# The first four chunks of a recurrence inverted in one batch, their loads first, and eight PSUM banks for attention until the first block

## The chip, the cores and the metric

The kernel runs on one core of one Trainium2 chip. Times are device microseconds of that core; the median of three runs is what is compared (before: 1098.84 us, runs from 1097.51 to 1099.29). Five engines work on one program, each with its own list of instructions that it takes strictly in order: PE (TensorE, matrix products), DVE (VectorE), ACT (ScalarE), POOL (GpSimd) and SP (SyncE, which here only issues DMAs). They wait for one another by semaphores.

## The reference

The output is three things in a row. First a recurrence over 768 steps for 4 x 8 heads, each with a state of 40 x 40; then two feed-forward layers over 3072 tokens of 320 numbers, with 2048 hidden units each.

```python
for t in range(S):                                    # S = 768, D = 40
    y[:, :, t] = einsum('bhd,bhde->bhe', rt, state)
    Sa = einsum('bhde,bhe->bhd', state, at)
    state = state * wt[:, :, None, :] - einsum('bhd,bhe->bhde', Sa, bt) \
            + einsum('bhd,bhe->bhde', vt, kt)
x = y.transpose(0, 2, 1, 3).reshape(B * S, H * D)     # 3072 x 320
h = x @ w_in;  g = h * tanh(softplus(h));  x = g @ w_out   # first layer
h = x @ w_in;  g = h * cos(h);             out = g @ w_out # second layer
```

The weights of both layers come as 64-bit floats and are split in the kernel into a rounded part and a rest, so that each product of the layers is a sum of three matmuls: rounded input by rounded weight, rounded by rest, and rest by rounded.

## The kernel before, in words

**Recurrence.** The 768 steps are cut into 24 time chunks of 32 steps, and the heads into two halves of 16 units each. One half of one chunk is a piece g (g = 2 x chunk + half), 48 pieces in all. Inside a piece the recurrence is turned into products and the inverse of a triangular 32 x 32 matrix for each unit. A piece goes through these stages:

- `pre(g)`: the load of the inputs (IN, L564/L565), on DVE a running product of the decays (tile PE, L570), its reciprocal (D1R, L575, L576), scaled inputs (AM L584, KB L590); on PE the products of L607 and the transposes of L640; on DVE the masked results (AM, L617); a DMA stores the triangular matrix to DRAM (l_d, L630/L631).
- `inverse(bt)`: for a batch of pieces, 64 partitions for two pieces. DMA XM<-l_d (L667), then 28 dependent steps (L682 a product into XT, L680 a sum into XM; 14 of each), DMA t_d<-XM (L693), DMA TT<-t_d (L697). The steps of the first three batches are on DVE, those of later ones on POOL. All 24 batches have two pieces.
- `halves(bt)`: the two 16 x 16 blocks of each inverse are joined: TA on DVE (L724), products L719 and L721 on PE with TB (L727) between them, and a copy to TT.
- `chain(g)`: what must run from chunk to chunk, since each needs the state (SV) that the one before left: on PE the products rhs (L790), ztm (L813), zmm (L804), rvz (L862), fmm (L888) and the transposed state stm (L932); on DVE between them FR (L872), the new state SV (L899) and the output Y (L907); ACT copies RS, ZS and FL.

After two chunks, 64 steps by 4 sequences, 256 tokens are stored to DRAM (x_d, L951/L952) and make one block of the first layer.

**Layers.** Block: load XR (L1041 to L1043), rounded part XH on ACT (L1046), rest XL on DVE (L1048), hidden products h on PE (L991), activation on ACT (L1061, L1063), its rest GL on DVE (L1066), output products (L972). There are twelve such blocks, and the pieces' work runs beside them. The second layer (L1006 to L1149) comes after the last piece.

**Weights.** `prep` loads 64-bit pieces of the weights (TMP<-in_w_in, L454), ACT takes one part (L461), DVE another with two or three integer operations (L466, L471, L479), ACT or DVE writes the rounded weight (L390, L392), and POOL the rest (L508).

**Order.** A planner (`Plan`, lines 120 to 250) puts every instruction of every engine in order at build time: it simulates the engines with costs of its own, and among the work that could start it takes the lowest rank `prio`. Chains have the rank -1e4 + 10g, `pre` and `inverse` about -5e3 + 10g, the first layer 100 x block, the second layer's weights 5e3. Buffers are rings with fixed counts: PSUM's eight banks are four for attention (PA), two for h (PH) and two for outputs (PO). On the chip each engine then waits at each instruction until its inputs and its buffer are there, and all behind it in that engine's list wait too.

Of the kernel before, what the change touches and what calls it, by code (L numbers as in the profile page):

```python
# [19 lines left out]
C = 32  # L20
# [68 lines left out]
SP_SAFE = 1.0  # L89

# [8 lines left out]
class Plan:  # L99
# [23 lines left out]
    def run(self):  # L123
# [12 lines left out]
        port_free = 0.0  # L136
# [4 lines left out]
        while done < len(self.tasks):  # L141
# [88 lines left out]
            t.end = free[e] + (0.2 if t.lat is None else t.lat)  # L230
# [6 lines left out]
            for u in t.succ:  # L237
                for x in u.engs:
                    u.ready[x] = max(u.ready[x], free[e] + (HOP.get((e, x), 0.15) if t.lat is None else t.lat))
# [12 lines left out]
def body(ctx, tc, ins, out):  # L252
# [11 lines left out]
    BATCH = [(i, 2) for i in range(0, TOT, 2)]  # L264
# [141 lines left out]
    DMA_LAT = 3.0  # L406
# [6 lines left out]
    AHEAD_W = 6  # L413
# [8 lines left out]
    W1_AFTER = lambda: None  # L422
    W2_PRIO = 5e3
# [8 lines left out]
    def prep(layer, names, prio, after, stage, stage2, half):  # L432
# [7 lines left out]
        for (kind, k, cc), h, n in parts:  # L440
            late = kind == "out" and cc >= 5
            if late and t_sw is None:
# [12 lines left out]
                       preds=after + ([t_sw] if late else []) + loads[-AHEAD_W:][:1] * (len(loads) >= AHEAD_W),  # L455
                       acq=[(rring, (key, "r"))], lat=DMA_LAT + 1.5, prio=prio)
# [85 lines left out]
    Gev, KBe, scanT, ldma, ttld, tt_last, ytask = {}, {}, {}, {}, {}, {}, {}  # L542
    io, Sev, STev, chain_last = {}, {}, {}, {}
# [9 lines left out]
    def pre(g):  # L553
# [5 lines left out]
        pe, am, kb, rp = (lambda: PE_t[P.at(k("PE"))]), (lambda: AM_t[P.at(k("AM"))]), \  # L559
# [13 lines left out]
        t_sc = fifo("scan", P.add("DVE", 0.64, scan, preds=[t_ld, S_D], acq=[("PE", k("PE"))], prio=pr, port=True))  # L573
# [59 lines left out]
        ldma[g] = P.add("SP", 1.0, ldm, preds=t_gl, lat=DMA_LAT, prio=pr)  # L633
# [19 lines left out]
    def inverse(bt):  # L653
# [4 lines left out]
        rows = lambda: slice(64 * P.at(("X", bt)), 64 * P.at(("X", bt)) + 2 * n)  # L658
# [10 lines left out]
        t = P.add("SP", 1.0, ld, preds=[ldma[g0 + i] for i in range(cnt)] + [S_X], acq=[("X", ("X", bt))], lat=DMA_LAT, prio=pr)  # L669

        own = bt >= 3
        IE = G if own else V

# [17 lines left out]
        def st():  # L691
# [3 lines left out]
        t = P.add("SP", 1.0, st, preds=[t], rel=[("X", bt)], lat=DMA_LAT, prio=pr)  # L695
        t = P.add(
            "SP", 0.5, lambda: SP.dma_start(TT_t[P.at(("TT", bt))][:, 0:cnt * 4], t_d[bt].rearrange("(cg i) j t -> (i j) cg t", i=4)),  # L697
            preds=[t], acq=[("TT", ("TT", bt), cnt)], lat=DMA_LAT, prio=pr)
        t = halves(bt, t)
        for i in range(cnt):  # L700
            ttld[g0 + i] = t

    def halves(bt, t):

        g0, cnt = BATCH[bt]
# [66 lines left out]
    def chain(g):  # L772
# [142 lines left out]
        sevs, yevs = [], []  # L915
        for h, ft in ((0, f0), (1, f1)):
            s = []
            if not last:
                s = [P.add("DVE", 0.315, sev(h, p), preds=[ft, io[nx][2]], prio=pr) for p in range(2)]
            sevs += s  # L920
            rel = [k(f"F{h}")] + ([k("PE")] if h == 1 else [])
            y_acq = [("Y", ykey)] if (yc == 0 and h == 0) else []
            yevs.append(P.add("DVE", 0.26, yev(h), preds=[ft] + s + yevs, acq=y_acq, rel=rel, prio=pr + 1))
# [22 lines left out]
        if yc == 1:  # L946
# [7 lines left out]
            ytask.setdefault(yb, []).append(P.add("SP", 1.0, yst, preds=yevs, rel=[ykey], lat=DMA_LAT, prio=pr))  # L954
# [79 lines left out]
    def layer1(blk, wready):  # L1034
        pr0 = blk * 100
        xk = ("x1", blk)
        xr = lambda: XR_t[P.at((xk, "xr"))]

# [6 lines left out]
        t = P.add("SP", 1.5, ld, preds=ytask[blk] + [blk_prev[0]], acq=[("XR", (xk, "xr"))], lat=DMA_LAT, prio=pr0)  # L1045
# [297 lines left out]
```

## Time and profile before

| what | value |
|---|---|
| runs | 1097.51 to 1099.29 us, median 1098.84 us |
| the profiled execution | 1094.35 us |
| its span, first to last instruction | 1092.6 us |
| PE, DVE, ACT, POOL busy | 92%, 68%, 50%, 40% of the span |
| granted TensorE clock, mean | 0.990 of 2.4 GHz |
| first product of the first layer | 132.96 us |
| first output product of the first layer | 142.4 us |
| last product of the chain | 590.6 us |

Times inside a row are microseconds from the start of the span. The profiled execution is 1.75 us longer than its span and 4.5 us shorter than the median of the runs. Shares over the whole span mix three parts: a start in which PE is busy a third of the time, a middle with attention and the first layer together, and the second layer alone.

### The profile page before, as it was taken

The page shows a single profiled execution, that of the slowest core. Times are in us where ns is not written, and L with a number is a line of the kernel's source. Part 1 is how long each engine was busy: PE and PEld are TensorE (multiplying, and loading weights), DVE is VectorE, ACT ScalarE, POOL GpSimd, SP SyncE. Part 2 cuts the span into 40 slices and gives each one's busy share as a digit, 9 for nine tenths or more (in the row PEclk, how much of TensorE's full clock was granted, in tenths as well). Part 3 has the DMA queues.
Part 4 walks back from the last instruction along what each step waited for, and adds up shares of the span by engine and source line. Part 5 has one row for each costly group of instructions (what it writes and reads, how often), then busy time and mean ns, then how long its engine had stood idle before and what let it go on. Part 6 is the DMA issues. An engine that isn't in the chain of part 4 may idle for free.

```text
span 1092.6 us, 36346 instructions
## 1 busy us (share of the span) xinstructions
PE 1008.8 (92%) x14888; PEld 926.3 (85%) x14888; DVE 743.6 (68%) x1661; ACT 545.2 (50%) x1346; POOL 437.3 (40%) x887
## 2 busy tenths in 40 slices
PE   2266899999999999999999999999999999999996
PEld 1255798898988898889999999999999999999996
DVE  8999887778677677678643987445555555565553
ACT  3255666655565565646565444444343434343433
POOL 5215267552463754365530332103333333333332
PEclk9999799999999999999999999999999999999999
DMA  8555564646545555555443442211100202010101
GB/s 239 152 152 159 158 179 126 170 121 178 143 127 159 142 157 144 147 151 156 107 130 110 142 143 86 86 46 30 42 13 1 54 1 53 1 39 1 25 1 25
DMA packets 109367, 111.88 MB, mean 102 GB/s; under 512 B 64145, under 2 KB 88721, under 8 KB 109201
## 3 DMA queue, kind: packets, MB, share of 16 engines
q1 hardware_dynamic: 109200, 109.57, 36.9%
q8 instruction: 117, 1.92, 0.8%
q14 instruction: 50, 0.40, 0.1%
HBM read 91.43 MB, written 18.09 MB: 100 GB/s over the span
## 4 chain that ended last, share of the span: by engine, by line
PE 62%; DVE 12%; issue 11%; POOL 6%; DMA 5%; ACT 4%; SPq 1%; POOLq 0%; DVEq 0%; ACTq 0%
PE bank L991 15%; PE bank L972 15%; PE bank L1006 8%; PE bank L1022 7%; POOL GL L1149 4%; PE bank L888 4%; PE bank L862 2%; PE bank L607 1%; PE bank L932 1%; PE bank L836 1%; PE bank L640 1%; DVE SV L899 1%; PE bank L790 1%; PE bank L804 1%; PE bank L719 1%
## 5 line engine op out<-in xcount | busy, mean ns | idle before, releaser
L1149 POOL TENSOR_TENSOR GL<-H,GH 128x512 fp32r<-128x512 f32 x96 | 124.5, 1297 | 238.2 <-ACT GH L1147 228.5
L682 POOL TENSOR_TENSOR XT<-XM 64x14 f32<-64x14 f32 (+6 forms) x294 | 102.2, 348 | 176.2 <-DMA XM<-l_d 155.3
L390 ACT ACTIVATE FL<-bank 64x160 f32<-64x160 f32 (+1 forms) x376 | 101.7, 295 | 87.4 <-PE bank L932 47.1
L1140 ACT ACTIVATE T<-T,half_pi 128x512 f32<-128x512 f32 x96 | 69.5, 723 | 113.8 <-DVE T L1137 113.8
L1133 DVE TENSOR_SCALAR T<-bank 128x512 f32<-128x512 f32 x96 | 66.4, 692 | 78.5 <-PE bank L1006 65.2
L1066 DVE TENSOR_TENSOR GL<-H,GH 128x512 fp32r<-128x512 f32 x96 | 70.7, 740 | 70.8 <-ACT GH L1063 70.2
L680 POOL TENSOR_TENSOR XM<-XM,XT 64x14 f32<-64x14 f32 (+6 forms) x294 | 106.1, 361 | 22.5
L1061 ACT ACTIVATE H<-bank 128x512 f32<-128x512 f32 x96 | 57.5, 599 | 105.4 <-PE bank L991 104.7
L1142 DVE TENSOR_TENSOR H<-bank,T 128x512 f32<-128x512 f32 x96 | 66.1, 689 | 53.0 <-ACT T L1140 52.2
L1147 ACT ACTIVATE GH<-H 128x512 fp32r<-128x512 f32 x96 | 60.6, 631 | 73.1 <-DVE H L1142 71.0
L991 PE MATMUL bank<-XH,wih 128*128 128x256 f32 x448 | 94.4, 293 | 0.5 <-ACT GH L1063 0.4
L991 PE MATMUL bank<-XH,wil 128*128 128x256 f32 x448 | 89.4, 281 | 0.0
L991 PE MATMUL bank<-XL,wih 128*128 128x256 f32 x448 | 89.1, 281 | 0.0
L607 PE MATMUL bank<-AM,KB 104*64 104x64 f32 x768 | 36.9, 246 | 48.1 <-DVE KB L590 39.6
L617 DVE TENSOR_TENSOR AM<-bank,maskG 64x128 f32<-64x128 f32 x192 | 55.1, 287 | 31.4 <-PE bank L607 20.2
L607 PEld LDWEIGHTS bank<-AM,KB 104*64 104x64 f32 x768 | 30.5, 155 | 52.5 <-issue 38.6
L991 PEld LDWEIGHTS bank<-XH,wih 128*128 128x128 f32 x448 | 69.8, 191 | 2.5 <-ACT GH L1063 0.8
L991 PEld LDWEIGHTS bank<-XL,wih 128*128 128x128 f32 x448 | 69.1, 190 | 1.0 <-issue 1.0
L991 PEld LDWEIGHTS bank<-XH,wil 128*128 128x128 f32 x448 | 69.3, 191 | 0.0
L991 PE MATMUL bank<-XH,wix 128*128 128x256 f32 x224 | 67.4, 301 | 0.9 <-issue 0.9
L1137 DVE SCALAR_TENSOR_TENSOR T<-T,bank 128x512 f32<-128x512 f32 x96 | 65.7, 684 | 2.2
L888 PE MATMUL bank<-FR,FL 104*64 104x72 f32 x1536 | 63.7, 240 | 3.6 <-ACT wih L390 2.0
(171 smaller groups left out, 2929.5 us busy)
## 6 DMA issues: line engine op xcount, KB each, us to landing
VR<-in_vR_dram SPq DMA_DIRECT2D x96, 160.0 KB
IN<-in_inT_dram SPq DMA_DIRECT2D x94, 161.4 KB
FR<-in_rI_dram SPq DMA_DIRECT2D x48, 180.0 KB
FR<-in_vF_dram SPq DMA_DIRECT2D x48, 144.0 KB
TMP<-in_w_in_dram SPq DMA_DIRECT2D x12, 512.0 KB
RA<-in_w_in_dram SPq DMA_DIRECT2D x12, 512.0 KB
RA<-in_w_out_dram SPq DMA_DIRECT2D x10, 512.0 KB
SV<-in_vS_dram SPq DMA_DIRECT2D x96, 52.0 KB
```

The costliest lines, as they stand in the source:

```text
L390: A.activation(o, i, AF.Copy)
L607: PE.matmul(gp[c0:c0 + 64, q // 2], kb()[:, q].rearrange("p a t -> p (a t)"), am()[0:104, :, q], start=True, stop=True)
L680: IE.tensor_tensor(out=b[:, 0:i, i + 1:16], in0=b[:, 0:i, i + 1:16], in1=tv, op=ALU.add)
L682: IE.tensor_tensor(out=tv, in0=bc(b[:, i:i + 1, i + 1:16], (2 * n, i, w)), in1=bc(b[:, 0:i, i:i + 1], (2 * n, i, w)), op=ALU.mult)
L888: PE.matmul(fp[64 * p:64 * p + 64, qp], fl()[0:104, n * D:n * D + 64], fr()[:, n], start=True, stop=True)
L972: PE.matmul(o, l[:, f, tsl], r, start=(first and f == 0 and i == 0), stop=(last and f == 1 and i == 2))
L991: PE.matmul(hp[:, f], pss[i][0], pss[i][1], start=(i == 0), stop=(i == 7))
L1006: PE.matmul(bank[P.at((key, "h"))][:, 0:512], pss[i][0], pss[i][1], start=(i == 0), stop=(i == 7))
L1022: PE.matmul(o, l, r, start=(ft == 0 and i == 0), stop=(ft == NFF - 1 and i == 2))
L1066: gl = P.add(GLE, (dve(512),), lambda eng, Hv=Hv, key=key: EN[eng].tensor_tensor(out=GL_t[P.at((key, "gl"))], in0=Hv(), in1=GH_t[P.at((key ...
L1140: c = P.add("ACT", act(512, False, 1), lambda f=f, Tv=Tv: A.activation(Tv(f), Tv(f), AF.Sin, scale=-TWO_PI, bias=half_pi), preds=[b], aset ...
L1149: gl = P.add("POOL", pool(512), lambda f=f, Hv=Hv, key=key: G.tensor_tensor(out=GL_t[P.at((key, "gl"))], in0=Hv(f), in1=GH_t[P.at((key, "g ...
```

## The change

- **Batches.** The first inverse takes four pieces (128 partitions), the others two as before: 23 inverses in place of 24. The first two (`OWN`) are on DVE, the rest on POOL. `halves` and the tile TT still take two pieces each, so the first inverse has two TT loads. Its four `pre` come first in the program.
- **Loads.** The inputs of the first pieces stand first in SP's list. Each weight load waits in the planner for an input load (the first four) or for the third TT load (the others), and only two weight loads may be open at a time in place of six. The state, FR and VR loads of a piece wait in the planner for those of the piece before. The planner's latency of a DMA is now worked out from its size in a queue (`kb`, `RATE`, `LAND`).
- **Banks.** Attention has all eight PSUM banks until the load of the first layer's first block; four of them then go to PH and PO. The piece g = 7 keeps its tile PE in an output buffer of the first layer.
- **Ranks.** The load, XH and XL of block 0 get the rank -9.955e3, that of the chains; Y goes ahead of SV in the pieces of chunk 1.

```diff
-    BATCH = [(i, 2) for i in range(0, TOT, 2)]
+    BATCH = [(0, 4)] + [(i, 2) for i in range(4, TOT, 2)]
...
-                 ("PA", 4), ("PH", 2), ("PO", 2)):
+                 ("PA", 8), ("PH", 0), ("PO", 0)):
...
-    AHEAD_W = 6
+    OWN = 2
+    AHEAD_W = 2
+    W1_FREE = 4
...
-                       preds=after + ([t_sw] if late else []) + loads[-AHEAD_W:][:1] * (len(loads) >= AHEAD_W),
-                       acq=[(rring, (key, "r"))], lat=DMA_LAT + 1.5, prio=prio)
+                       preds=(after if layer == 2 else [tt_ld[2]] if len(loads) >= W1_FREE else [t_in[2]]) + ([t_sw] if late else []) + (loads[-AHEAD_W:][:1] * (len(loads) >= AHEAD_W) if len(loads) >= W1_FREE else loads[-1:]),
+                       acq=[(rring, (key, "r"))], kb=0.5 * n, prio=prio)
...
-        t_ld = fifo("ld", P.add("SP", 1.0, ld, preds=[S_IN[2]] if g == 1 else S_IN[0:2], acq=[] if g == 1 else [("IN", k("IN"))], lat=DMA_LAT + 1.5, prio=pr))
+        t_ld = P.add("SP", 0.8, ld, preds=[S_IN[(0, 2, 1)[g]]] if g < 3 else [t_in[g - 1]], acq=[] if g == 1 else [("IN", k("IN"))], kb=500, prio=pr if g > 3 else g - 1e6)
...
-        own = bt >= 3
+        own = bt >= OWN
...
+        prx = -9.955e3 if blk == 0 else pr0
...
-        t = P.add("SP", 1.5, ld, preds=ytask[blk] + [blk_prev[0]], acq=[("XR", (xk, "xr"))], lat=DMA_LAT, prio=pr0)
+        t = P.add("SP", 1.5, ld, preds=ytask[blk] + [blk_prev[0]], acq=[("XR", (xk, "xr"))], kb=384, prio=prx)
+        if blk == 0:
+            for i, r in enumerate(("PH", "PO", "PH", "PO")):
+                P.add("SP", 0.0, lambda i=i, r=r: P.grow(r, [P.at(("bank", i))], P.time), preds=[t],
+                      acq=[("PA", ("bank", i))], lat=0.0, prio=-1e6)
         th = P.add("ACT", act(768, False), lambda: A.activation(XH_t[P.at((xk, "xh"))], xr(), AF.Copy), preds=[t],
-                   acq=[("XH", (xk, "xh"))], prio=pr0)
+                   acq=[("XH", (xk, "xh"))], prio=prx)
...
     state_init = {}
+    for g in range(4):
+        pre(g)
+    inverse(0)
     for g in range(TOT):
+        if g > 3:
+            pre(g)
         load_step(g)
-        pre(g)
-        if BT_OF[g][1] == BATCH[BT_OF[g][0]][1] - 1:
+        if g > 3 and BT_OF[g][1] == BATCH[BT_OF[g][0]][1] - 1:
             inverse(BT_OF[g][0])
```

On PE, between the chains of chunk 0 and chunk 1, the kernel before has this (L888 is the last product of chunk 0 and L932 its transposed state, L790 the first product of chunk 1, TT_232 the inverse of chunk 1, L719 and L721 the halves):

```order
L888 MATMUL bank_145<-FR_221,FL_209 64x72 x8
L888 MATMUL bank_147<-FR_221,FL_209 64x72 x8
L790 MATMUL bank_144<-SV_218,AM_203 32x40 x16
L932 MATMUL bank_146<-ident,SV_219 104x40 x4
L932 MATMUL bank_144<-ident,SV_219 104x40 x4
L790 MATMUL bank_145<-SV_219,AM_204 32x40 x16
L607 MATMUL bank_147<-AM_201,KB_217 64x64 x8
L640 MATMUL bank_146<-ident,KB_217 128x104 x4
L719 MATMUL bank_144<-TA,TT_232 32x32 x32
L721 MATMUL bank_144<-TT_232,TB 32x16 x32
L813 MATMUL bank_145<-TT_232,RS_234 40x32 x2
```

The changed kernel has this in the same place (TT_230 is the inverse of chunk 1; its L742, the second half, stands further up, beside the chain of chunk 0):

```order
L742 MATMUL bank_142<-TT_230,TB 32x16 x32
L960 MATMUL bank_146<-ident,SV_216 104x40 x4
L960 MATMUL bank_147<-ident,SV_216 104x40 x4
L910 MATMUL bank_148<-FR_219,FL_207 64x72 x8
L910 MATMUL bank_149<-FR_219,FL_207 64x72 x8
L812 MATMUL bank_143<-SV_216,AM_201 32x40 x16
L620 MATMUL bank_144<-AM_199,KB_215 64x64 x8
L960 MATMUL bank_145<-ident,SV_217 104x40 x4
L960 MATMUL bank_142<-ident,SV_217 104x40 x4
L835 MATMUL bank_146<-TT_230,RS_232 40x32 x2
```

The halves of chunk 1 have moved from between L790 and L813 of chunk 1 (now L812 and L835) to the chain of chunk 0.

On DVE, around the rest XL of block 0, the kernel before has this (L570 to L590 are `pre` of pieces far ahead, RL is the second part of the output weights, GL the first rest of an activation):

```order
L575 RECIPROCAL D1R<-PE_198 104x8
L576 SCALAR_TENSOR_TENSOR RP_215<-IN_192,D1R 104x264
L584 TENSOR_TENSOR AM_205<-IN_192,PE_198 40x256
L1048 TENSOR_TENSOR XL_187<-XR_184,XH_185 128x768
L617 TENSOR_TENSOR AM_204<-bank_146,maskG 64x4x32 x4
L466 TENSOR_SCALAR RL_236<-RL_236 128x256
L471 SCALAR_TENSOR_TENSOR RL_236<-RL_236 128x256
L466 TENSOR_SCALAR RL_237<-RL_237 128x256
```

The changed kernel has this (SV and Y are state and output of chunk 2, H the staging of weights):

```order
L479 SCALAR_TENSOR_TENSOR H_177<-TMP,H_177 128x512
L474 TENSOR_SCALAR H_176<-H_176 128x512
L921 TENSOR_TENSOR SV_217<-bank_143,PE_197 40x4x40 x2
L921 TENSOR_TENSOR SV_217<-bank_145,PE_197 40x4x40
L1081 TENSOR_TENSOR XL_185<-XR_182,XH_183 128x768
L921 TENSOR_TENSOR SV_217<-bank_145,PE_197 40x4x40
L929 TENSOR_TENSOR Y_237<-bank_143,PE_197 104x4x32
```

XL of block 0 has moved 59 rows up in DVE's list, to row 228 from row 287, and stands between two parts of a chain's state. The first GL is row 276 in place of row 299.

On SP, just ahead of the load XR of block 0, the changed kernel has this (TMP is a weight load, IN the inputs of a later piece):

```order
L979 DMA x_d_57<-Y_237 40x4x128
L980 DMA x_d_57<-Y_237 40x4x128
L763 DMA FR_219<-in_rI_dram 40x1152
L764 DMA FR_219<-in_vF_dram 32x1152
L773 DMA SV_216<-in_vS_dram 32x416
L774 DMA SV_216<-in_vS_dram 32x416
L462 DMA TMP<-in_w_in_dram 128x1024 x2
L573 DMA IN_191<-in_inT_dram 40x1033
L574 DMA IN_191<-in_inT_dram 40x1033
L1070 DMA XR_182<-x_d_57 128x2x256
```

The load now has two weight loads and an input load between itself and the store x_d, and each of these waits for a buffer that DVE frees.

## Rows read from the trace of the kernel before

**Rows 1.** Stretches of the span: us; busy PE, PEld, DVE, ACT, POOL; PEclk, DMA, GB/s.

```profile
0.00:60.00 60.00, 17.10 (x342) 13.87 (x344) 54.59 (x146) 19.24 (x46) 22.06 (x58) 1.00 0.67 190
60.00:133.00 73.00, 53.56 (x1388) 45.54 (x1380) 65.88 (x186) 41.62 (x122) 25.11 (x49) 0.93 0.60 165
...
175.00:600.00 425.00, 414.32 (x9418) 375.43 (x9417) 295.25 (x785) 250.68 (x746) 205.25 (x595) 1.00 0.54 143
```

**Rows 2.** What PE waited for, 0 to 150 us: total us, times, longest.

```profile
PE bank L607 <- DVE KB L590: 39.6, 5, 17.0
```

**Rows 3.** Timeline of PE between the chains of chunks 0 and 1: start, us.

```profile
77.08 0.76 PE L790 MATMUL bank<-SV,AM 96*32 96x40 f32 x32
92.29 0.76 PE L813 MATMUL bank<-TT,RS 32*40 32x32 f32 x32 [0.56 <-ACT TT L390]
```

**Rows 4.** Timeline of DVE, XL and first GL of block 0.

```profile
131.21 0.96 DVE L1048 TENSOR_TENSOR XL<-XR,XH 128x768 fp32r<-128x768 f32 x1
139.44 0.69 DVE L1066 TENSOR_TENSOR GL<-H,GH 128x512 fp32r<-128x512 f32 x1
```

**Rows 5.** Timeline of PE, first h and outputs of block 0.

```profile
132.96 0.80 PE L991 MATMUL bank<-XH,wih 128*128 128x256 f32 x2
136.20 0.39 PE L991 MATMUL bank<-XH,wih 128*128 128x256 f32 x2
142.80 0.31 PE L972 MATMUL bank<-woh1a,GL 128*128 128x320 f32 x1
```

**Rows 6.** Lines of DVE, 0 to 94.5 us: busy, mean ns, idle before.

```profile
L680 DVE TENSOR_TENSOR XM<-XM,XT 64x14 f32<-64x14 f32 (+6 forms) x42 | 10.9, 261 | 1.1
L682 DVE TENSOR_TENSOR XT<-XM 64x14 f32<-64x14 f32 (+6 forms) x42 | 10.1, 240 | 1.1
```

**Rows 7.** One tile's instructions, first 20 us: ns min/median/max, first and last start.

```profile
L365 DVE TENSOR_TENSOR TB<-lowd x1: 168/168/168, 11.0 to 11.0; 128x8 f32<-128x8 f32 x1
```

**Rows 8.** Lines of DVE by form, whole span.

```profile
L899 DVE TENSOR_TENSOR SV<-bank,PE 40x160 f32<-40x160 f32 x184 | 58.9, 320 | 5.8 <-PE bank L888 1.3 <-ACT GH L1063 1.2
L590 DVE TENSOR_TENSOR KB<-IN,RP 104x256 f32<-104x256 f32 x94 | 41.5, 454 | 2.4 <-PE bank L640 2.1
...
L872 DVE TENSOR_TENSOR FR<-bank,maskR 64x256 f32<-64x256 f32 x96 | 38.9, 419 | 29.9 <-PE bank L862 13.8 <-ACT GH L1063 6.9 <-ACT VR L390 3.9
L907 DVE TENSOR_TENSOR Y<-bank,PE 104x128 f32<-104x128 f32 x96 | 26.8, 283 | 1.6 <-PE bank L888 0.2
L471 DVE SCALAR_TENSOR_TENSOR RL<-RL 128x256 uint32<-128x256 uint32 x10 | 4.1, 422 | 0.1
L466 DVE TENSOR_SCALAR RL<-RL 128x256 uint32<-128x256 uint32 x10 | 2.9, 302 | 5.6 <-ACT RL L461 5.6
```

**Rows 9.** Lines of POOL, 0 to 133 us.

```profile
L508 POOL TENSOR_TENSOR wil<-H,wih 128x512 fp32r<-128x512 f32 x8 | 12.5, 1566 | 29.9 <-ACT wih L390 29.8
```

**Rows 10.** Timeline of POOL and DVE: one subtraction and the instruction beside it.

```profile
108.20 1.51 POOL L508 TENSOR_TENSOR wix<-H,GH 64x512 fp32r<-64x512 f32 x1
108.58 1.42 DVE L590 TENSOR_TENSOR KB<-IN,RP 104x256 f32<-104x256 f32 x1
```

**Rows 11.** SP and ACT, load and rounding of block 0.

```profile
115.00 0.45 SPq L1041 DMA_DIRECT2D XR<-x_d  x1
120.54 0.84 ACT L1046 ACTIVATE XH<-XR 128x768 fp32r<-128x768 f32 x1 [1.80 <-DMA XR<-x_d]
```

**Rows 12.** Stretches of PE alone: us; busy; PEclk, DMA, GB/s.

```profile
126.00:134.00 8.00, 7.17 (x193) 0.50 0.68 193
```

**Rows 13.** Timeline of PE: last product of the chain, first transposes of layer two.

```profile
590.63 2.22 PE L888 MATMUL bank<-FR,FL 104*64 104x72 f32 x64
697.03 0.38 PE L1110 MATMUL bank<-ident,XR 128*128 128x128 f32 x2
```

**Rows 14.** Staging of the second layer's weights: ns min/median/max, first and last start.

```profile
L461 ACT ACTIVATE AU<-RA x22: 659/679/691, 600.3 to 712.9; 128x512 f32<-128x512 f32 x22
L508 POOL TENSOR_TENSOR wix<-AU,DG x4: 1296/1718/1730, 614.1 to 672.5; 64x512 fp32r<-64x512 f32 x4
```

More of the change, by code (lines that the diff above doesn't have):

```diff
@@ L89 @@
 SP_SAFE = 1.0
+RATE, LAND = 200.0, 1.6
 def mode_cost(a, b):
@@ L135, in run @@
         done = 0
-        port_free = 0.0
+        port_free, queue = 0.0, 1.5
         recent = []
@@ L229, in run @@
                 port_free = free[e]
-            t.end = free[e] + (0.2 if t.lat is None else t.lat)
+            lat = t.lat
+            if t.kb:
+                queue = max(queue, free[e]) + t.kb / RATE
+                lat = queue + LAND - free[e]
+            t.end = free[e] + (0.2 if lat is None else lat)
             for key in t.rel:
@@ L238, in run @@
                 for x in u.engs:
-                    u.ready[x] = max(u.ready[x], free[e] + (HOP.get((e, x), 0.15) if t.lat is None else t.lat))
+                    u.ready[x] = max(u.ready[x], free[e] + (HOP.get((e, x), 0.15) if lat is None else lat))
                 u.n_wait -= 1
@@ L571, in scan @@
                                  data1=D1.rearrange("p q t -> p (q t)"), initial=0.0, op0=ALU.mult, op1=ALU.add)
-        t_sc = fifo("scan", P.add("DVE", 0.64, scan, preds=[t_ld, S_D], acq=[("PE", k("PE"))], prio=pr, port=True))
+        t_sc = fifo("scan", P.add("DVE", 0.64, scan, preds=[t_ld, S_D], acq=[] if g == PX else [("PE", k("PE"))], prio=pr, port=True))
+        scanT[g] = t_sc
         def rscan():
@@ L657, in inverse @@
         n = cnt * NU
-        rows = lambda: slice(64 * P.at(("X", bt)), 64 * P.at(("X", bt)) + 2 * n)
+        slots = [("X", bt, i) for i in range((cnt + 1) // 2)]
+        r0 = lambda: 64 * min(P.at(i) for i in slots)
+        rows = lambda: slice(r0(), r0() + 2 * n)
         x = lambda: XM[rows(), 0:528]
@@ L667, in ld @@
                 SP.dma_start(part(h), dr(l_d, h))
-        t = P.add("SP", 1.0, ld, preds=[ldma[g0 + i] for i in range(cnt)] + [S_X], acq=[("X", ("X", bt))], lat=DMA_LAT, prio=pr)
-        own = bt >= 3
+        t = P.add("SP", 1.0, ld, preds=[ldma[g0 + i] for i in range(cnt)] + [S_X], acq=[("X", i) for i in slots], kb=64 * cnt, prio=pr)
+        own = bt >= OWN
         IE = G if own else V
+        inv_ld[bt] = t
         def step(i, add):
@@ L693, in st, with halves @@
                 SP.dma_start(dr(t_d, h), part(h))
[L695 to L705, printed above, removed]
+        t = P.add("SP", 1.0, st, preds=[t], rel=slots, kb=64 * cnt, prio=pr)
+        tv = t_d[bt].rearrange("(cg i) j t -> (i j) cg t", i=4)
+        for g in range(g0, g0 + cnt, 2):
+            key, two, o = ("TT", g // 2), min(2, g0 + cnt - g), 4 * (g - g0)
+            th = P.add("SP", 0.5, lambda key=key, two=two, o=o: SP.dma_start(
+                TT_t[P.at(key)][:, 0:4 * two], tv[:, o:o + 4 * two]),
+                preds=[t], acq=[("TT", key, two)], kb=128 * two, prio=pr)
+            tt_ld[g] = th
+            th = halves(g, two, th)
+            for i in range(two):
+                ttld[g + i] = th
+    def halves(g0, cnt, t):
+        bt = g0 // 2
         G4 = 4 * cnt
@@ L915, in chain @@
         sevs, yevs = [], []
+        early = c == 1
         for h, ft in ((0, f0), (1, f1)):
             s = []
-            if not last:
+            rel = [k(f"F{h}")] + ([k("PE")] if h == 1 and g != PX else [])
+            y_acq = [("Y", ykey)] if (yc == 0 and h == 0) else []
+            if early:
+                yevs.append(P.add("DVE", 0.26, yev(h), preds=[ft] + yevs, acq=y_acq, prio=pr - 30))
+                for p in range(2):
+                    s.append(P.add("DVE", 0.315, sev(h, p), preds=[yevs[-1], io[nx][2]] + s, rel=rel if p else [], prio=pr))
+            elif not last:
                 s = [P.add("DVE", 0.315, sev(h, p), preds=[ft, io[nx][2]], prio=pr) for p in range(2)]
             sevs += s
-            rel = [k(f"F{h}")] + ([k("PE")] if h == 1 else [])
-            y_acq = [("Y", ykey)] if (yc == 0 and h == 0) else []
-            yevs.append(P.add("DVE", 0.26, yev(h), preds=[ft] + s + yevs, acq=y_acq, rel=rel, prio=pr + 1))
+            if not early:
+                yevs.append(P.add("DVE", 0.26, yev(h), preds=[ft] + s + yevs, acq=y_acq, rel=rel, prio=pr + 1))
         Sev[g] = sevs
@@ L1168, in store @@
                     SP.dma_start(out[r0:r0 + 64], OB_t[P.at(ok)][64 * i:64 * i + 64])
-            P.add("SP", 1.0, store, preds=[o], rel=[ok], lat=DMA_LAT, prio=pr0)
-    S_IN = [P.add("DVE", 1.1, lambda i=i: setup_in(i), prio=-1e6) for i in range(3)]
+            P.add("SP", 1.0, store, preds=[o], rel=[ok], kb=164, prio=pr0)
+    S_IN = {}
+    for i, p in ((0, None), (2, 0), (1, 2)):
+        S_IN[i] = P.add("DVE", 1.1, lambda i=i: setup_in(i), preds=[S_IN.get(p)], prio=-1e6)
     S_D = P.add("DVE", 0.7, setup_d, prio=-9.5e5)
@@ L1201, in body @@
         chain(g)
+    P.add("SP", 0.0, lambda: P.grow("OB", [1], P.time), preds=[chain_last[PX]], lat=0.0, prio=-1e6)
     for blk in range(12):
@@ L1224, in switch @@
             P.grow(r, range(len(STG[r])), P.time)
-        P.grow("PH", [0, 1], P.time)
-        P.grow("PO", [2, 3], P.time)
+        rest = sorted(i for _, i in P.rings["PA"])
+        P.grow("PH", rest[0:2], P.time)
+        P.grow("PO", rest[2:4], P.time)
     def half2():
```

42 lines of the change are left out of this document (22 added, 20 removed).

## The prediction

> **What bounds the kernel now.** I read the stretches first. Up to 133 us DVE is busy for 54.6 of 60 and 65.9 of 73 us, PE for 17.1 and 53.6; from 175 to 600 us PE is busy for 414.3 of 425 us [rows 1]. So there are two limits: until the first layer's first h, DVE's list; after it, PE's work. A change at the start is worth what it brings forward the moment at which PE has enough to do, counted in PE work already done at that moment. Then I read what PE waits for in the first 150 us: 39.6 us of it are waits for KB, that is for DVE in `pre` [rows 2]. The timeline shows the shape of it: after rhs of chunk 1 at 77.08 us the next chain product, ztm, starts at 92.29, since the inverse of chunk 1 (its own batch before) and its halves come between [rows 3]. Last I read when the first layer begins: XL of block 0 runs at 131.21, h starts at 132.96, the first GL is at 139.44, and its output product at 142.80 [rows 4, 5]. XR had been issued at 115.00 and XH began at 120.54 [rows 11]: XL stood 10 us behind its input, in DVE's order.
>
> **The change part by part.** The sum is made up to the first GL, because from there on PE is never short of work. DVE's list up to it has 276 rows in place of 299.
> - One inverse fewer on DVE: 28 steps. The 84 steps of before took 10.9 + 10.1 us [rows 6], 0.25 us each: -7.0 us. That the steps are now 128 partitions wide costs nothing: a product over 128 partitions and 8 columns took 0.168 us, as short as the smallest steps on 64 [rows 7]. The bounds: all steps of the wide inverse as now (0), or, since no row shows this step at 128, up to as long as two narrow ones (+7.0). I take 0, the nearer row.
> - Two weight jobs RL later: each 0.30 + 0.42 + 0.42 us [rows 8], -2.3 us. One AM and one KB later, about 0.45 each [rows 8]: -0.9 us.
> - More chain in that list: 4 FR of 0.42, 8 SV of 0.32, 4 Y of 0.28 [rows 8]: +1.7 + 2.6 + 1.1 = +5.4 us.
> - Together -4.8 us. DVE stood still for 12.5 us in the two stretches [rows 1] and was stretched besides (below). With eight banks and the inputs ahead of the weights I expect these losses to shrink, but the later loads of weights open new ones; bounds -8 to +5 us, taken -1.2. So the first GL comes 6.0 us earlier, at about 133.4.
> - In before PE used the first GL 3.4 us after it began, 2.7 after it ended [rows 4, 5], being busy with h and chain. In the new order h of block 0 begins just behind fmm of g = 5, and PE waits for GL: -2.7, rounded with the handover to about -3.
> - The same moment has more PE work behind it. In the order before the first output product the changed kernel has 32 more fmm, 32 rhs, 16 stm and 8 h, 8 fewer L607 and 8 L640. A product of fmm takes 0.069 us (2.22 us for 64 records, two records to a product [rows 13]), and in the same way I read 0.026 for rhs, 0.04 for stm, 0.12 for h, 0.08 for L607 and 0.115 for L640 from the timeline at full clock: 2.2 + 0.8 + 0.6 + 0.9 - 0.6 - 0.9, an estimate of 3.0 us: -3.0.
>
> The sum is 6.0 + 3 + 3.0 = 12 us.
>
> A walk from the other end agrees. The first inverse now waits for `pre` of four pieces, so the chain of chunk 0 starts later, by my count some 4 us. But chunk 1 has its inverse already, its halves stand beside chunk 0, and the 14.5 us between 77.84 and 92.29 [rows 3] fall away: chunk 1 ends about 10 us earlier. XL of block 0 then runs at 105 to 107 us, 25 earlier than before; yet GL needs the weights that DVE makes between, and it is the list that decides it.
>
> **Loads and queue.** XR is issued at row 100 of SP's list, behind two weight loads that wait for staging buffers and one input load that waits for its ring. From its issue to XH took 5.54 us, XH 0.84 [rows 11], so XL could run 6.5 us after the issue. DVE's list behind XL holds SV and Y of the chain, and all of it waits if XR is late. Worth nothing if the issue comes by 99.5 us; this is the third rival. The weights of outs and h now load later and in pairs; their price is within the losses above.
>
> **DVE beside POOL.** On this trace 1.42 us for one KB stood beside a POOL subtraction of 1.51 us begun 0.38 before [rows 10], where KB has a mean of 0.45 [rows 8]. By my count of the timeline about 12 DVE instructions were stretched so, 10 us in all, beside 17 subtractions, 8 of which are in [rows 9]. The Trainium skill ("SBUF — State Buffer", Who interferes with whom) says that a DVE instruction with two SBUF inputs and a GpSimd instruction reading SBUF exclude each other fully. The pairing in the row agrees; that every subtraction meets such an instruction no row shows, and that case is the fifth rival.
>
> **Rivals.**
> 1. Larger gain. DVE's losses (12.5 us of idling and the 10 us of stretching) mostly go, since PE no longer keeps it waiting: GL at 122 to 126, total about 20 us; profiled 1074, 1078.5 on the median. For: half of DVE's list is prepared early and eight banks leave L607 free to run ahead. Against: the POOL subtractions stay.
> 2. The start's gain is given back. The chain's last product comes later in PE's order: half a block more of h stands ahead of it. Between 592.85 and 697.03 [rows 13] the second layer's weights are split, from 600.3 to 674 us for what its first block needs [rows 14]: 74 of the 104 us there. I estimate half a block of layer 1 at 17 to 19 us; 85 are left, so it just fits. If it doesn't, or if the reshuffled middle costs as much as it gains, the time stays within 0.2%: about 1098.
> 3. Slower, by one mechanism: XR late. XL of block 0 stands in DVE's list at row 228 in the middle of a chain. If the weight loads ahead of XR on SP wait for rows of DVE that are late, XR is issued at 120 instead of 99.5. DVE then stands until 126.5 with some 48 rows (about 22 us) to go to GL, which comes at about 149: 10 us later than before; less the 3 us of PE work that lie behind it, 1094.35 + 7 = 1101, 1106 on the median. It decides from an issue at about 113 on, where GL comes when it does now. For: in before XR was issued at 115.00 [rows 11]. Against: it waited there for the chain that now ends 10 us earlier.
> 4. The clock. In before PE ran at a granted 0.50 from 126 to 134 us [rows 12], the 1.2 GHz level, after holes; the first two h took 0.80 us, later 0.39 [rows 5]. Now there is a hole between h of block 0 and GL. If PE falls to 0.50 there, the outputs of the first stretch run at half speed, about 5 us: gain 7, 1092. The Trainium skill ("TensorE: Matmul & The Clock Gate", What's actually happening) has idleness gate the array to half rate; by it this is likely for a part, and the trace's 0.50 behind holes agrees.
>
> 5. The subtractions. If each of the 17 now meets a DVE instruction of the chain, the loss is 17 x 0.97 (1.42 less 0.45 [rows 8, 10]) = 16.5 us in place of 10, and the gain 12 - 6.5 = 5.5: 1088.9 profiled, 1093 on the median. For: the weights come later, into the chain's stretch. Against: they are no more than before, and met such an instruction 12 times in 17 already.
>
> **In the middle** the orders differ little: at the first h of block 1 PE has done 1.4 us more than before, and DVE's list to the XL of block 1 is 319 rows in place of 354, of which 28 are the inverse. PE stands still for 10.7 us in 175 to 600 [rows 1]; I give the reshuffling 4 us either way.
>
> **How the numbers follow.** The profiled execution of 1094.35 less 12 is 1082.3. It lies 4.5 below the median of the runs; on that basis 1086.8, rounded to 1087. Chances: this forecast 0.40 (with 1082 to 1092), the larger gain 0.19, the clock 0.10, the subtractions 0.08, given back 0.10, late XR or another loss at the start 0.13. The range of 8 in 10 reaches from 1075, the larger gain with its uncertainty, to 1097, just short of no change. About 0.2% (2.2 us) is what a measurement of this kernel can tell from no change. Faster 0.78: the forecast, the larger gain, the clock and the subtractions make 0.77, and a part of the given-back case 0.01 more; same 0.10, most of given back and a little of the loss; slower 0.12.
>
> **What would show it.** Right: GL of block 0 near 133 us, its output product within a microsecond behind it; XL near 106 and no long stop on DVE before it; no gap on PE between rhs and ztm of chunk 1 like the one at 77.84; the 28 wide steps at 0.2 to 0.25 us each; the last fmm 0 to 6 us later than 590.6 with more of layer 1 done; the second layer's transposes at about 685. Wrong: XR issued after 113 us; the wide steps twice as long; waits of layer 2's first h for wih; DVE's stretched instructions twice as many.

## The result, and the profile after

The changed kernel takes 1102.45 us (median of 20 runs, 1096.84 to 1110.02) against 1096.76 us (20 runs, 1089.18 to 1104.90): ratio 1.0054, interval 1.0034 to 1.0073, some 6 us slower. Forecast was 12 us faster. Run once more beside the experiments it gave 1.004 (1.001 to 1.007). The profiled execution took 1100.16 us, its span is 1098.4 us.

The stretches of the changed kernel (columns as in [rows 1]), which answer to those rows, and DVE alone up to the first GL (columns: us; busy, instructions; PEclk, DMA share, GB/s):

```profile
0.00:60.00 60.00, 16.06 (x262) 13.11 (x265) 52.39 (x147) 14.16 (x40) 16.14 (x56) 1.00 0.51 136
60.00:80.00 20.00, 13.63 (x478) 12.32 (x469) 11.02 (x42) 8.07 (x25) 0.56 (x2) 1.00 0.64 205
80.00:133.00 53.00, 38.71 (x1026) 32.48 (x1016) 44.97 (x107) 35.51 (x98) 26.43 (x45) 0.67 0.67 192
133.00:147.00 14.00, 12.21 (x138) 10.64 (x138) 12.28 (x32) 7.51 (x18) 11.48 (x32) 0.50 0.49 144
175.00:200.00 25.00, 19.20 (x339) 17.41 (x340) 21.37 (x58) 13.70 (x41) 15.48 (x43) 0.86 0.62 177
...
0.00:146.60 146.60, 120.24 (x325) 0.84 0.59 166
```

The same two questions put to the kernel before give these rows:

```profile
60.00:80.00 20.00, 14.47 (x307) 12.42 (x299) 18.23 (x63) 11.75 (x35) 3.10 (x4) 1.00 0.58 168
175.00:200.00 25.00, 23.53 (x555) 20.73 (x555) 21.14 (x57) 16.95 (x48) 15.40 (x40) 1.00 0.52 136
...
0.00:139.40 139.40, 125.94 (x346) 0.95 0.62 172
```

DVE's work up to the first GL did shrink, by 125.94 - 120.24 = 5.7 us. But DVE stood still for 26.4 us of that time where it had stood for 13.5. Seven of the 13 lie between 60 and 80 us. What DVE waited for between 60 and 110 us in the changed kernel (total us, times, longest), and SP's weight loads up to 70 us with the first TT loads (start, us):

```profile
DVE AM L630 <- PE bank L620: 4.3, 1, 4.3
DVE TB L748 <- ACT FR L396: 3.2, 1, 3.2
DVE XT L699 <- DMA XM<-l_d: 2.6, 1, 2.6
DVE FR L894 <- PE bank L884: 2.3, 1, 2.3
```

```profile
41.58 0.45 SPq L462 DMA_DIRECT2D TMP<-in_w_out_dram  x1
52.32 1.02 SPq L716 DMA_DIRECT2D TT<-t_d  x2
58.54 0.91 SPq L462 DMA_DIRECT2D TMP<-in_w_out_dram  x2
64.19 0.83 SPq L462 DMA_DIRECT2D TMP<-in_w_in_dram  x2
```

These are short waits of a chain, of which every kernel here has some. What is missing is work to put into them: the load at 41.58 us is the fourth weight load, the next one comes 17 us later, behind TT. Before, 11 had been issued by 50 us, the last of them at 47.02. The TT load that holds them is that of pieces 2 and 3 (`tt_ld` goes by the piece), so the second TT load and not the third; both were issued at 52.32.

Each tile of the first layer's weights takes DVE one step L471 (L479 in the changed kernel) and one L466 (L474), 1.1 us together. All three kernels here do 17 of them up to 133 us. Up to 80 us they have done (before, changed, and e7, in which the hold is undone, see below):

```profile
L471 DVE SCALAR_TENSOR_TENSOR H<-TMP,H 128x512 uint32<-128x512 uint32 x9 | 6.1, 685 | 0.1
L479 DVE SCALAR_TENSOR_TENSOR H<-TMP,H 128x512 uint32<-128x512 uint32 x4 | 2.7, 681 | 0.0
L479 DVE SCALAR_TENSOR_TENSOR H<-TMP,H 128x512 uint32<-128x512 uint32 x9 | 6.0, 679 | 0.1
```

So five of the 17 have moved from the time before 80 us to the stretch behind it. The rest of the start (start, us, engine, line; of DVE, PE and SP apart):

```profile
116.83 0.94 DVE L1081 TENSOR_TENSOR XL<-XR,XH 128x768 fp32r<-128x768 f32 x1
121.00 1.49 DVE L603 TENSOR_TENSOR KB<-IN,RP 104x256 f32<-104x256 f32 x1
123.01 1.77 DVE L581 TENSOR_TENSOR_SCAN PE<-IN,D 104x264 f32<-104x264 f32 x1
146.64 0.68 DVE L1099 TENSOR_TENSOR GL<-H,GH 128x512 fp32r<-128x512 f32 x1
```

```profile
79.52 0.76 PE L812 MATMUL bank<-SV,AM 96*32 96x40 f32 x32
82.42 0.51 PE L835 MATMUL bank<-TT,RS 32*40 32x32 f32 x32
...
107.22 1.12 PE L620 MATMUL bank<-AM,KB 104*64 104x64 f32 x16
116.09 0.51 PE L1019 MATMUL bank<-XH,wih 128*128 128x256 f32 x2 [0.50 <-ACT XH L1079]
125.17 0.92 PE L740 MATMUL bank<-TA,TT 16*32 16x32 f32 x64 [3.66 <-DVE TA L745]
141.21 0.79 PE L1019 MATMUL bank<-XH,wih 128*128 128x256 f32 x2
150.27 0.47 PE L1000 MATMUL bank<-woh1a,GL 128*128 128x320 f32 x1
153.40 0.69 PE L620 MATMUL bank<-AM,KB 104*64 104x64 f32 x16
```

```profile
107.17 0.39 SPq L1070 DMA_DIRECT2D XR<-x_d  x1
```

Chunk 1's gap of 14.5 us between rhs and ztm [rows 3] is 2.1 us now (80.28 to 82.42), and h begins at 116.09, 17 us earlier than before [rows 5]. It stops at 121 and goes on at 141.21. That it ran out of columns with their weights ready fits the trace (ACT wrote `wih` at 119.54 and 120.78 and not again before 132.71), but no run isolates it.

To see how far PE was at a moment, I counted, from both traces, each line's matmul records up to that moment, and priced them at that line's mean in the kernel before between 175 and 590 us (ztm, whose records gave no price, is left out). An estimate, in us of PE work at full clock, ahead of the kernel before (+) or behind it (-):

| at (us) | 100 | 133 | 147 | 175 | 200 | 240 | 400 | 600 |
|---|---|---|---|---|---|---|---|---|
| changed | +2.9 | +3.8 | -3.3 | -6.7 | -13.7 | -15.1 | -9.1 | -8.7 |
| e7, weights not held for TT | +2.8 | +10.6 | +12.1 | +7.5 | +2.6 | -0.5 | +1.5 | +4.5 |
| e12, e7 with the late rank | +2.8 | -0.3 | -1.3 | -5.2 | -2.7 | -3.2 | -6.0 | -4.0 |
| e9, the hold in the kernel before | +5.1 | +6.8 | +1.1 | -1.7 | -6.0 | -8.3 | -15.4 | -18.1 |

The changed kernel loses in two places: between 121 and 150 us, and again between 175 and 200, where PE was busy for 19.2 of 25 us, at a granted clock of 0.86. The later ends: the last fmm begins at 599.29 us (590.63 before) and the first transposes of layer two at 702.21 (697.03) [rows 13].

### The profile page after: what moved, and what is told of

It reads as the page before. It is cut to its first block, busy times and chain, and to the rows that moved or that the text cites. A ratio compares the mean times of both kernels' runs of the same rounds, so it can differ in the third digit from the quotient of the medians.

```text
span 1098.4 us, 36306 instructions
## 1 busy us (share of the span) xinstructions
PE 1008.2 (92%) x14888; PEld 927.1 (84%) x14888; DVE 738.3 (67%) x1633; ACT 543.2 (49%) x1345; POOL 431.0 (39%) x887
## 5 line engine op out<-in xcount | busy, mean ns | idle before, releaser
L697 POOL TENSOR_TENSOR XM<-XM,XT 64x14 f32<-64x14 f32 (+6 forms) x294 | 102.1, 347 | 22.6
L1099 DVE TENSOR_TENSOR GL<-H,GH 128x512 fp32r<-128x512 f32 x96 | 68.5, 714 | 53.9 <-ACT GH L1096 52.6
L620 PE MATMUL bank<-AM,KB 104*64 104x64 f32 x768 | 38.0, 250 | 47.1 <-DVE KB L603 41.9
L620 PEld LDWEIGHTS bank<-AM,KB 104*64 104x64 f32 x768 | 31.4, 158 | 53.1 <-issue 45.6
L894 DVE TENSOR_TENSOR FR<-bank,maskR 64x256 f32<-64x256 f32 x96 | 39.2, 420 | 50.3 <-PE bank L884 17.8
L910 PEld LDWEIGHTS bank<-FR,FL 104*64 104x64 f32 x1536 | 57.5, 149 | 11.9 <-issue 5.3
```

The source lines that it names most:

```text
L620: PE.matmul(gp[c0:c0 + 64, q // 2], kb()[:, q].rearrange("p a t -> p (a t)"), am()[0:104, :, q], start=True, stop=True)
L697: IE.tensor_tensor(out=b[:, 0:i, i + 1:16], in0=b[:, 0:i, i + 1:16], in1=tv, op=ALU.add)
L910: PE.matmul(fp[64 * p:64 * p + 64, qp], fl()[0:104, n * D:n * D + 64], fr()[:, n], start=True, stop=True)
L1099: gl = P.add(GLE, (dve(512),), lambda eng, Hv=Hv, key=key: EN[eng].tensor_tensor(out=GL_t[P.at((key, "gl"))], in0=Hv(), in1=GH_t[P.at((key ...
```

## The experiments

All ran with five rounds; the ratio is to the kernel before on the same chip. I compared two theories: W, that the first layer's weights are held back, DVE has nothing to fill its waits with, and the weights come behind the chain; C, that an early h of block 0 leaves holes in which PE's clock falls, and that this is the cost.

**e1, e7: the hold on the weight loads undone.** Both take away the wait for TT. e1 lets six loads be open, in both layers; e7 keeps two open. Both also let the first four loads overlap, which in the changed kernel go one at a time:

```diff
-preds=(after if layer == 2 else [tt_ld[2]] if len(loads) >= W1_FREE else [t_in[2]]) + ... + (loads[-AHEAD_W:][:1] * (len(loads) >= AHEAD_W) if len(loads) >= W1_FREE else loads[-1:]),
+preds=(after if layer == 2 else [t_in[2]]) + ... + loads[-6:][:1] * (len(loads) >= 6),     # e1
+preds=(after if layer == 2 else [t_in[2]]) + ... + loads[-2:][:1] * (len(loads) >= 2),     # e7
```

> The changed kernel with one part undone: a weight load of the first layer waits in the planner only for the third input load, and six may be open, as before; all else as changed. Theory W (the late weights are what was mis-sized: DVE has nothing to fill its waits with between 60 and 80 us and the first layer's weights come after the chain): DVE busy at least 16 of the 20 us from 60 to 80 (11.0 in the changed kernel, 18.2 before), first GL at 138 us or earlier (146.6 changed), time 4 to 9 us below the changed kernel, about 0.997 of before. Theory C (PE runs at 1.2 GHz from 120 to 152 us because block 0's h is let in too early): GL not before 143 us, granted clock still about 0.5 from 133 to 147, time within 3 us of the changed kernel.

> The changed kernel with the weight loads no longer held for the third TT load, but with two open at a time as changed. Theory W with the wait for TT as its cause: most of what six open loads and no wait gave, 5 to 9 us below the changed kernel. Theory W with the number of open loads as its cause: within 3 us of the changed kernel.

e1: 0.997 (0.9947 to 0.9993), its first GL at 137.01. e7: 0.9916 (0.9886 to 0.9945), 1089.63 us median against 1096.66: some 9 us faster than before and 13 to 15 faster than the changed kernel. More than expected. The number of open loads is not the cause, since e7 keeps two; the wait for TT and the one-at-a-time order of the first four were not tried apart. The stretches of e7, its first GL, and DVE alone up to it:

```profile
60.00:80.00 20.00, 13.44 (x470) 11.80 (x470) 16.91 (x47) 12.56 (x32) 9.40 (x7) 1.00 0.80 220
120.00:133.00 13.00, 12.02 (x308) 10.96 (x299) 9.87 (x27) 11.69 (x31) 3.72 (x6) 1.00 0.53 132
133.00:147.00 14.00, 14.00 (x264) 12.94 (x265) 12.93 (x36) 8.90 (x28) 11.47 (x35) 1.00 0.67 194
```

```profile
126.14 0.69 DVE L1099 TENSOR_TENSOR GL<-H,GH 128x512 fp32r<-128x512 f32 x1
...
0.00:126.10 126.10, 107.31 (x294) 0.99 0.66 180
```

DVE is busy for 16.9 of the 20 us from 60 to 80 where the changed kernel had 11.0; POOL subtracts in the same 20 us (9.4 in place of 0.6); the first GL comes 20 us earlier, and PE is busy without a stop from 133 to 147 us, at a granted 1.00. e7 beats both kernels. Filled waits are only part of those 20 us: DVE's idle time up to the first GL falls from 26.4 to 18.8, by 7.6, and its work ahead of GL from 120.24 to 107.31, by 12.9, since the planner's new order puts fewer steps of chain and `pre` ahead of it.

**e9: the hold put into the kernel before**, and nothing else of the change:

```diff
-preds=after + ([t_sw] if late else []) + loads[-AHEAD_W:][:1] * (len(loads) >= AHEAD_W),
+preds=after + ([tt_ld[0]] if layer == 1 and len(loads) >= 4 else []) + ([t_sw] if late else []) + (loads[-2:][:1] if layer == 1 and len(loads) >= 4 else loads[-AHEAD_W:][:1] * (len(loads) >= AHEAD_W)),
```

> The kernel before with one part of the change added: from the fifth weight load of the first layer on, a load waits in the planner for the first TT load (47.5 us there) and two may be open; batches, banks, ranks and other loads as before. Theory W (holding the weights is the loss by itself): DVE busy under 16 of the 20 us from 60 to 80 (18.2 before) or first GL after 143 us (139.4 before), time 5 to 12 us above before, ratio 1.005 to 1.011. If the wait only hurts together with the batch of four: within 3 us of before.

1.0139 (1.0098 to 1.018), 14 to 15 us slower: the size of e7's step, with the other sign, above the range that was expected. The hold here is both the wait for TT and two open loads in place of six; 4 loads were issued by 50 us in place of 11. The stretches (the last row is the kernel before) and the first GL of e9:

```profile
60.00:80.00 20.00, 13.90 (x318) 11.92 (x314) 17.92 (x66) 8.71 (x26) 3.17 (x4) 1.00 0.73 201
...
100.00:120.00 20.00, 15.24 (x437) 13.38 (x434) 13.19 (x31) 10.67 (x30) 7.66 (x25) 0.69 0.65 178
...
100.00:120.00 20.00, 17.09 (x420) 14.47 (x416) 17.93 (x42) 11.00 (x33) 11.07 (x25) 1.00 0.56 148
```

```profile
144.60 0.69 DVE L1068 TENSOR_TENSOR GL<-H,GH 128x512 fp32r<-128x512 f32 x1
```

Here DVE was full from 60 to 80 (my mark for theory W was wrong in its place) and stood still between 100 and 120, 13.2 of 20 where before had 17.9. So it is not one stretch that the hold empties. But the first GL is only 5.2 us later than before (144.60 against 139.44), a third of the loss. The table shows e9 ahead by 1.1 us at 147, behind by 8.3 at 240 and by 18.1 at 600; why it goes on losing there is open.

**e2: the batch of four undone.**

```diff
-    BATCH = [(0, 4)] + [(i, 2) for i in range(4, TOT, 2)]
-    OWN = 2
+    BATCH = [(i, 2) for i in range(0, TOT, 2)]
+    OWN = 3
```

> The changed kernel with one part undone: 24 inverses of two pieces, the first three on DVE; loads, banks and ranks as changed. Theory W: the batch of four is a gain by itself (28 steps of 0.22 us and an earlier chunk 1), so without it the time is 3 to 7 us above the changed kernel, about 1.010 of before. Theory B (the batch of four is the loss, because chunk 0 waits for four pieces' inputs): 4 to 8 us below the changed kernel, level with before.

1.0141 (1.0117 to 1.0166): slower than the changed kernel by some 9 us, so the batch of four is a gain in the company of the hold and the early rank, larger than the 3 to 7 expected. Four executions only; without the hold it was not tried.

**e3, e12: the rank of block 0 undone**, in the changed kernel (e3) and in e7 (e12):

```diff
-        prx = -9.955e3 if blk == 0 else pr0
+        prx = pr0
```

> The changed kernel with one part undone: load, XH and XL of block 0 have the first layer's rank again, so that h of block 0 stands behind more of the chain; all else as changed. Theory C (h too early, holes behind it, half clock): granted clock over 0.7 from 133 to 147 us (0.50 changed), time 4 to 8 us below the changed kernel. Theory W: PE still waits for the weights, the first GL stays within 3 us of 146.6, time within 3 us of the changed kernel.

> The kernel without the wait for TT (e7), with the load, XH and XL of block 0 at the first layer's rank. With the weights there in time an early block 0 can be used: theory W expects the rank to be worth 2 to 6 us now, ratio 0.994 to 0.998. If early h only leaves holes at half clock (theory C): within 2 us of e7 or below it.

e3: 1.0033 (1.0016 to 1.0051), within 3 us of the changed kernel, first GL at 144.98, granted clock 0.62 from 133 to 147 (over 0.7 was expected of theory C): theory C's gain of 4 to 8 us isn't there. But h began at 121.32 in place of 116.09, so the rank moved it by only 5 us. e12: 1.0051 (1.0026 to 1.0076), some 15 us slower than e7 where 2 to 6 were expected. XL and first GL of e12:

```profile
128.19 0.95 DVE L1081 TENSOR_TENSOR XL<-XR,XH 128x768 fp32r<-128x768 f32 x1
153.64 0.68 DVE L1099 TENSOR_TENSOR GL<-H,GH 128x512 fp32r<-128x512 f32 x1
```

Together with e5 and e7 these are four corners:

| | weights held | weights not held |
|---|---|---|
| early rank | 1.004 to 1.0054 | 0.9916 |
| late rank | 1.0033 | 1.0051 |

The rank is worth 15 us when the weights are there, and about nothing when they are not. Read the other way, taking the hold away gains 13 to 15 us with the early rank and nothing that shows with the late one. So neither is the cost or the gain by itself here: it is early h together with early weights that pays. Why the hold costs 14 to 15 us in the kernel before, which has the late rank too (e9), the runs don't say.

**e10: the banks undone** (four for attention, two for h, two for outputs from the start).

```diff
-                 ("PA", 8), ("PH", 0), ("PO", 0)):
+                 ("PA", 4), ("PH", 2), ("PO", 2)):
```

> The changed kernel with one part undone: four banks for attention, two for h and two for outputs from the start; weights held as changed. Theory W: the banks are neither the gain nor the loss, first GL within 4 us of 144 to 147, time within 4 us of the changed kernel (ratio 1.001 to 1.009). If giving the banks to attention is part of the loss: under 1.000.

1.0035 (1.0012 to 1.0057), not to be told from the changed kernel (the first GL was at 152.39, later than expected). In this company the eight banks bring nothing that shows. Nor does the first GL alone order the times: e10 has it 6 us later than the changed kernel at the same time, e11 below 6 us earlier than before at 1.0025.

**e4, e6, e8: matmuls that keep PE busy.** Unused products of the first weights, in e4 ahead of the halves of chunk 3, in e6 with 15 more ahead of its second half, in e8 in e1 ahead of an fmm of chunk 2:

```diff
+                if i == 0 and g0 == 6:
+                    for _ in range(30):
+                        PE.matmul(pa(k)[:, 256:512], W[1][0][:, 0, 0:128], W[1][0][:, 0, 0:256], start=True, stop=True)
                 for n in range(cnt * NU):
```

> The changed kernel with 30 more matmuls of 128x128 by 256 columns in PE's list ahead of the halves of chunk 3 (L740 at 125.2 us), where PE stood still from 121.5 to 125.2; they take about 3.4 us at 2.4 GHz and their result is not used. Theory C: they keep the clock at 2.4 GHz, granted clock over 0.8 from 122 to 130 us and over 0.6 from 133 to 147; the time falls by 3 to 6 us. Theory W: PE is not the limit there, DVE and the weights are; the clock may be higher but the first GL stays within 2 us of 146.6, and the time within 2 us of the changed kernel.

> The changed kernel with the 30 unused matmuls ahead of L740 of chunk 3 and 15 more ahead of its L742 (some 1.6 us of PE at 2.4 GHz). Theory C (the clock costs the time from 120 to 152 us): 4 to 8 us below the changed kernel, granted clock over 0.8 from 120 to 140 us. Theory W alone (late weights, the clock only follows): within 2 us of the changed kernel or up to 2 us above it.

> The kernel with early weight loads (no wait for TT, six open), and 28 unused matmuls of 256 columns ahead of the last product of the first piece of chunk 2 (L910 at 97.1 us there, behind a hole of 2.9 us), about 3 us of PE at 2.4 GHz. There PE ran at 0.50 from 92 to 132 us, busy for most of it. Theory C: the clock is over 0.7 from 97 to 120 us, first GL 3 us or more earlier than 137.0, time 2 to 6 us below the kernel with early weights. Theory W: clock or not, DVE sets the pace there: time within 2 us of it.

e4: 0.9989 (0.9968 to 1.001), 5 to 7 us below the changed kernel; but its profiled execution (1099.95 us, 7 above its median) shows the first GL at 146.30 and 0.50 from 133 to 147 like the changed kernel, though 1.00 from 122 to 130 as theory C asked. e6: 1.003 (0.9997 to 1.0063), like the changed kernel, with a granted 0.88 from 120 to 140 in its profiled execution where the changed one had 0.64: the mark of theory C for the clock was met and its gain of 4 to 8 us wasn't there. The two times don't agree, and the clock's own share stays open: e4's gain would be the whole loss against the kernel before, e6's is none. e8: 0.9935 (0.9907 to 0.9962) against 0.997 for e1, with intervals that overlap; the first GL came 2.5 us earlier (134.52), less than the 3 expected of theory C.

**e5: the changed kernel again.**

> The changed kernel once more, unchanged, so that it stands beside the others on the same chip. Both theories: 1.003 to 1.008 of before, that is 3 to 9 us above it.

1.004 (1.001 to 1.007), as expected.

**e11: a third inverse on DVE in e7.**

```diff
-    OWN = 2
+    OWN = 3
```

> The kernel without the wait for TT (e7), with a third inverse, that of chunk 3, on DVE in place of POOL. With the weights early, PE was 12 us of work ahead of before at 147 us and level with it at 240, and its waits in between were for TA and TB, which wait for inverses that POOL runs between subtractions. If POOL's inverse sets the pace of chunk 3 on: PE keeps 4 us or more of the 12 at 240, time 2 to 5 us below e7 (ratio 0.987 to 0.990). If DVE, which gets 28 steps more, is the limit: 2 to 6 us above e7.

1.0025 (0.9992 to 1.0057), 11 to 12 us slower than e7, where 2 to 6 were expected if DVE is the limit. That fits DVE, with 28 steps more ahead of the first GL (133.04 in place of 126.14), as the limit there, and not POOL's inverse; the size is not accounted for. What takes e7's 12 us back between 147 and 240 us is not settled.

## Why the prediction was wrong

**The step that failed** is "I expect these losses to shrink, but the later loads of weights open new ones; bounds -8 to +5 us, taken -1.2". Measured: +12.9 us (26.4 less 13.5 of idle DVE). The forecast GL of 133.4 plus this 14.1 is 147.5; it came at 146.64. The later weights had been seen and put "within the losses above" without pricing them by themselves. The trace of before would have allowed it: 9 of the 17 weight tiles were split by 80 us, and the hold leaves loads for four. e7 and e9 show from both sides that the hold costs time; by which path is shown in part only: in e7 idle time is 7.6 of the 20.5 us by which GL moves, and the four corners show that the cost hangs on the early rank.

The second term, -3 because PE would wait for GL and use it at once, failed as well: PE used GL at 150.27, 3.6 us after it began, where before had 3.4 [rows 4, 5]. The third held: by the count of the table PE had done 55.4 us of work at that moment, against 51.5 in before, so 3.9 more (forecast 3.0). The sum as it came is 7.2 later, 0.3 later and 3.9 of work more: 3.6 us behind in place of 12 ahead.

**The list came out right, in part by luck.** DVE's work to the first GL fell by 5.7 us (forecast 4.8). The steps of the inverses saved more than the 7.0 forecast: 84 took 21.0 us [rows 6], the 56 that are left took 11.0, so 10.0. The rest of the list grew by 4.3 where 2.2 was forecast, and the two misses nearly cancel. The wide steps cost what narrow ones do, 216 ns against 210 at 56 elements; of the 28 on each line, half are at 128 partitions:

```profile
L699 DVE TENSOR_TENSOR XT<-XM 128x14 f32<-128x14 f32 (+13 forms) x28 | 5.5, 196 | 3.4 <-DMA XM<-l_d 2.6
L697 DVE TENSOR_TENSOR XM<-XM,XT 128x14 f32<-128x14 f32 (+13 forms) x28 | 5.5, 196 | 0.8
...
L699 DVE TENSOR_TENSOR XT<-XM 128x56 f32<-128x56 f32 x2 | 0.4, 216 | 0.1
L699 DVE TENSOR_TENSOR XT<-XM 64x56 f32<-64x56 f32 x2 | 0.4, 210 | 0.1
```

**"From there on PE is never short of work" was wrong as well.** In 175 to 200 us PE stood still for 5.8 us (1.5 in before), of which 4.5 were waits for `pre`, which DVE did late; and from 190.4 to 197.2 us it ran at a granted 0.50, which makes the 0.86 of that stretch. Such a row has to be read against the order (waits; then the instructions of PE and DVE):

```profile
PE bank L620 <- POOL XT L699: 4.5, 2, 3.4
```

```profile
191.03 1.12 PE L620 MATMUL bank<-AM,KB 104*64 104x64 f32 x16 [3.37 <-POOL XT L699]
```

```profile
190.49 0.39 DVE L603 TENSOR_TENSOR KB<-IN,RP 104x256 f32<-104x256 f32 x1
```

The releaser named is POOL, but L620 reads KB, and KB ended on DVE at 190.88, 0.15 us before L620 began.

**The rivals.** The larger gain has its start in e7 (GL at 126.14, at the end of the 122 to 126 named), and there +12.1 us of PE work were measured at 147, though the time gained was 9. The late XR took no part: it was issued at 107.17, before the 113 that was to decide, and DVE didn't stand for XL. It was 8 us later than the 99.5 hoped for, though, and XL ran at 116.83 where the walk from the other end had 105 to 107. The slower end came by another mechanism than the one I had priced. The clock did fall, as the fourth rival said: granted 0.50 from 133 to 147, and L620 took 1.12 us at 107.22 and 0.69 at 153.40. PE's hole ahead of that fall, 3.66 us up to 125.17, was a wait for TA, which DVE began at 124.70 behind weight steps, the KB of 1.49 and the scan of 1.77 us shown above. Whether the clock or the late weights cost more is not settled, and e3 hardly moved h. The subtractions were no more in DVE's way than before by number: single instructions stretched beyond 1.05 us are 8 up to the first GL, 9 before; but that KB and that scan, both beside a subtraction, are two of the 8. The Trainium skill ("SBUF — State Buffer", Who interferes with whom) has a DVE instruction with two SBUF inputs and a GpSimd instruction that reads SBUF exclude each other; the trace agrees for those pairs, and 15 subtractions up to the first GL gave 8 of them. The start was given back in part later too, as in the second rival, but at 175 to 240 us; the second layer's weights, split from 624 us on, held nothing up there that shows: from the last fmm to the transposes it took 102.9 us, 106.4 before.

## What to carry to other kernels

Work that fills an engine's waits is worth the waits that it fills: before holding back its loads, look what else that engine would do, and price the hold by a term of its own: the engine's idle time, and what the new order puts ahead of the step that counts. Edits with one aim can depend on each other: the early rank of block 0 was worth 15 us with its weights there and nothing without, and freeing the weights was worth nothing without the early rank. A count of work done at chosen moments, priced from one kernel's rows, shows where a lead is won and lost when the end alone says little.

## What the runs showed that was not expected

The same kernel spreads over more than 1% on one core: the changed one from 1096.84 to 1110.02 us, the one before from 1089.18 to 1104.90. One profiled execution can lie 7 us from the median (e4), so a small difference between two traces is not a difference between two kernels. And the granted clock is shown as 1.00 where a stretch has no record of it: in two executions of the changed kernel the row for 80 to 100 us reads 0.61 and 1.00, with PE busy 14.49 and 14.77 us. The first record lies at 118.7 us in the kernel before and at 81.2 in the changed one, so the 1.00 of the rows for 0 to 60 and 60 to 80 us says nothing about the clock. The durations do:

```profile
110.79 1.12 PE L607 MATMUL bank<-AM,KB 104*64 104x64 f32 x16
118.60 0.69 PE L607 MATMUL bank<-AM,KB 104*64 104x64 f32 x16
```

In the kernel before the same 16 records took 1.12 us at 110.79, inside a row that reads 1.00, and 0.69 at 118.60: PE was at the lower of its two levels, 1.2 GHz, there too. So both kernels ran part of their start at it: ztm of chunk 1 took 0.76 us at 92.29 in before [rows 3], and in the changed kernel rhs took 0.76 at 79.52 and ztm 0.51 at 82.42. Of the stretches recorded at 0.50 before 160 us, the last ended at 135.8 us in before, at 152.8 in the changed kernel and at 120.0 in e7.
